# Later exps of q and a bank cycle of four in chunk 0 of an attention-plus-MLP kernel

## The chip, the cores and the metric

The kernel runs on one core of a Trainium2 chip. The metric is the device time of one execution in microseconds (us), as a median over runs. The span in a profile is the same execution without its launch, about 2 us shorter than its time.

## The reference, cut to what matters

```python
# attention, per batch b of 8 and head h of 8, S = 576, D = 64
q_s = softmax(q, axis=-1)            # exp, row sum, divide
k_s = softmax(k, axis=2)
kv  = einsum('bhsd,bhse->bhde', k_s, v)
x   = einsum('bhsd,bhde->bhse', q_s, kv)     # 4608 tokens x 512
# MLP
h   = x @ w_in                        # 512 -> 2048
out = (h * sigmoid(h)) @ w_out        # 2048 -> 512
```

Inputs and output are float32; the kernel multiplies in fp16 and bf16.

## The kernel before

The tokens go through in nine chunks. Chunk 0 makes 16 blocks of 128 features; each block is 8 matmuls into a set of two PSUM banks, then a tanh on ScalarE and a multiply on VectorE which frees the set. There are four sets, named by their first bank: 4, 0, 2 and 6.

```python
WIDE = (4, 0, 2, 6) * 3 + (4, 2, 0, 6)          # bank set of block 0..15

def wide_silu(fb):                               # tanh on ScalarE, multiply on VectorE
    bank = WIDE[fb]
    silu(0, fb, PS[:, bank:bank + 2, 0:S // 2], GTS[0][:, fb, :]..., S)
...
wide_mm(0, (0, 1))                               # first halves of blocks 0, 1, 2 ahead of
xt_evac(0, 1, 6, 0, 320, 0, nc.scalar)           # the second half of x
xt_evac(0, 1, 2, 0, 256, 320, nc.vector)
wide_mm(1, (0, 1))
wide_mm(2, (0, 1))
...
# plan(u, f): f is issued ahead of unit u; units 0..15 are the blocks of chunk 0, b1 = 16
plan(9,  lambda: (load_w2(8, 12), exp_q(1, 0, 0, 1)))
plan(10, lambda: (exp_q(1, 0, 1, 2), qsum_pair(1, 0)))      # qsum_pair: two adds on GpSimd
plan(12, lambda: (exp_q(1, 1, 0, 1), qsum_end(1, 0)))       # qsum_end: reduction on VectorE
plan(13, lambda: (exp_q(1, 1, 1, 2), qsum_pair(1, 1), qnorm(1, 0, nc.gpsimd)))
plan(b1, lambda: (qsum_end(1, 1), qnorm(1, 1, nc.vector)))
...
# joining batch 1: v is cast, k^T v ("kv") multiplied, scaled by VectorE, multiplied with q
plan(b1 + 3, lambda: (ws_op(1, 1), ws_op(2, 1)))            # ws_op: sums of w_in blocks, VectorE
plan(b1 + 4, lambda: ws_op(3, 1))
plan(b1 + 5, lambda: (vcast(1, 1, nc.scalar, 0, 1), vcast(1, 1, nc.vector, 1, 2)))
plan(b1 + 6, lambda: ws_op(4, 1))
plan(b1 + 7, lambda: kv_both(1))                            # kv matmuls, reciprocal, scaling
plan(b1 + 8, lambda: xt(1, 0))                              # "the kv product": q times scaled kv
```

Units from b1 on are the second product, which reads w_out in 16 blocks of 128 rows.

The softmax here doesn't subtract the row's maximum and nothing guards it: scores larger than these inputs give would overflow.

## Time and profile before

| | before |
|---|---|
| median of 3 runs | 261.32 us (261.06 to 261.46) |
| span, TensorE busy | 260.3 us, 251.3 us |
| longest wait of TensorE between the start of chunk 0 and the last stage | 0.8 us near 28 us, for a multiply of VectorE |

A timeline line reads: start in us, length in us, engine, source line, operation, output <- input, shapes, count; in brackets the idle time of the engine before it and what ended it. Some names: PS is the PSUM, sg a tanh's result, GT the product of VectorE's multiply, qt and vt the loaded q and v, eq the exp of q, vaug the cast v, kvn the scaled kv, WS a weight sum. The lines themselves stand in the prediction below.

### The profile page before, as it was taken

To read this page: it belongs to the slowest core of one execution; us is meant where nothing else is said; L and a number is where in the kernel's file an instruction comes from. 1 tells how busy PE (TensorE), PEld (TensorE's weight loads), DVE (VectorE), ACT (ScalarE), POOL (GpSimd) and SP (SyncE) were. 2 spreads that over 40 slices of the span, in tenths; PEclk is the share of its full clock that TensorE was granted. 3 is DMA by queue.
4 is the path that set the end of the run, shared out by engine and by line. 5 is a ranking of instruction groups with operands and counts; after the bars stand their busy time and mean duration, and the time that the engine had idled before them with its cause. 6 is when DMAs were issued, how large, how long until landed. Compare 5 with 4: busy or idle time off the path is not lost.

```text
span 260.3 us, 6411 instructions
## 1 busy us (share of the span) xinstructions
PE 251.3 (97%) x2732; PEld 203.4 (78%) x2732; DVE 208.0 (80%) x268; ACT 187.5 (72%) x212; POOL 65.8 (25%) x63
## 2 busy tenths in 40 slices
PE   8799899999999999999999999999999999999992
PEld 3467656656888888888888888888888888888881
DVE  2867797998997999799979997999798548855932
ACT  5765978998993899489948995799573848484610
POOL 1743791650460306030603060306000000000003
PEclk9999999999999999999999999999999999999999
DMA  6999999679999585956694869530433003300624
GB/s 247 335 196 297 302 320 330 260 159 393 271 343 230 140 246 191 232 128 170 268 249 112 229 216 213 139 83 3 91 81 83 3 0 82 81 3 1 140 64 121
DMA packets 35964, 45.89 MB, mean 176 GB/s; under 512 B 16208, under 2 KB 21008, under 8 KB 35936
## 3 DMA queue, kind: packets, MB, share of 16 engines
q1 hardware_dynamic: 29568, 33.69, 47.5%
q0 software_dynamic: 6128, 11.60, 17.3%
q8 instruction: 21, 0.34, 0.6%
q10 hardware_dynamic: 240, 0.20, 0.2%
q14 instruction: 7, 0.06, 0.1%
HBM read 36.70 MB, written 9.44 MB: 177 GB/s over the span
## 4 chain that ended last, share of the span: by engine, by line
PE 66%; DVE 3%; POOL 1%; issue 0%; ACT 0%; POOLq 0%; DVEq 0%; ACTq 0%
PE PS L477 34%; PE PS L377 30%; PE PS L234 2%; DVE h L355 1%; PE PS L195 1%; DVE GT L451 1%; POOL out_dram L740 1%; DVE zq L154 0%; DVE ow L725 0%; ACT sc L493 0%; DVE ow L497 0%; DVE rzq L158 0%; POOLq L856 0%; DVE kvn L208 0%; DVE rz L206 0%
## 5 line engine op out<-in xcount | busy, mean ns | idle before, releaser
L355 DVE TENSOR_TENSOR h<-PS,h 128x1024 f32<-128x1024 f32 (+1 forms) x45 | 54.0, 1199 | 12.7 <-ACT h L89 6.3
L477 PEld LDWEIGHTS <-GT 128*128 128x128 f16 x512 | 49.6, 98 | 6.9 <-issue 1.2
L377 PEld LDWEIGHTS <-WS 128*128 128x128 f16 x480 | 46.8, 98 | 6.2 <-issue 0.5
L477 PE MATMUL PS<-W,GT 128*128 128x256 f16 x384 | 49.1, 273 | 0.0
L377 PE MATMUL PS<-XS,WS 128*128 128x256 f16 (+1 forms) x360 | 46.3, 272 | 0.1
L361 ACT ACTIVATE GT<-h 128x1024 f16<-128x1024 f32 (+1 forms) x45 | 46.1, 1047 | 0.1
L89 ACT COPY h<-PS 128x1024 f32<-128x1024 f32 (+1 forms) x35 | 35.1, 1003 | 13.1 <-PE PS L377 12.6
L163 POOL TENSOR_TENSOR eq<-eq,rzq 128x1152 bf16<-128x1152 bf16 x13 | 27.7, 2133 | 53.7 <-DVE rzq L158 53.3
L477 PEld LDWEIGHTS <-S 128*128 128x128 f16 x384 | 37.2, 98 | 5.2 <-issue 1.0
L377 PEld LDWEIGHTS <-W 128*128 128x128 f16 x360 | 34.7, 98 | 4.7 <-issue 0.2
L477 PE MATMUL PS<-T,S 128*128 128x256 f16 x256 | 32.7, 273 | 0.0
L377 PE MATMUL PS<-XT,W 128*128 128x256 f16 (+1 forms) x240 | 29.5, 272 | 0.0
L361 ACT ACTIVATE GT<-PS 128x1024 f16<-128x1024 f32 (+1 forms) x15 | 15.2, 1016 | 18.9 <-PE PS L377 18.9
L91 POOL CAST vaug<-vt 128x1152 bf16<-128x1152 f32 x12 | 14.8, 1240 | 44.4 <-DMA vt<-in_v_dram 36.0
L108 ACT ACTIVATE eq<-qt 128x1152 bf16<-128x1152 f32 (+1 forms) x18 | 19.1, 1059 | 3.3 <-DMA qt<-in_q_dram 3.2
L740 POOL DMA_DIRECT2D out_dram<-ow x5 | 2.7, 547 | 72.3 <-DVE ow L725 72.3
L113 ACT ACTIVATE ek<-kt 128x1152 bf16<-128x1152 f32 x16 | 18.4, 1153 | 1.4 <-DMA kt<-in_k_dram 1.4
L154 DVE TENSOR_REDUCE zq<-eq 128x18 f32<-128x1152 bf16 x12 | 16.1, 1345 | 3.8 <-ACT eq L108 3.8
L267 PE MATMUL PS<-XT,W 128*128 128x288 f16 x128 | 16.2, 286 | 0.8 <-DVE GT L257 0.8
L477 PE MATMUL PS<-W,S 128*128 128x256 f16 x128 | 16.5, 273 | 0.0
L497 DVE SCALAR_TENSOR_TENSOR ow<-PS,sc 128x512 f32<-128x512 f32 x7 | 4.8, 692 | 14.4 <-ACT sc L493 14.4
L267 PEld LDWEIGHTS <-W 128*128 128x128 f16 x128 | 12.4, 98 | 4.6 <-issue 1.2
(79 smaller groups left out, 346.7 us busy)
## 6 DMA issues: line engine op xcount, KB each, us to landing
out_dram<-ow SPq DMA_DIRECT2D x64, 128.0 KB, 2.4
qt<-in_q_dram SPq DMA_DIRECT2D x12, 576.0 KB, 4.7
kt<-in_k_dram SPq DMA_DIRECT2D x12, 576.0 KB, 5.6
vt<-in_v_dram SPq DMA_DIRECT2D x12, 576.0 KB, 5.4
qt<-in_q_dram POOLq DMA_DIRECT2D x4, 576.0 KB, 10.8
kt<-in_k_dram POOLq DMA_DIRECT2D x4, 576.0 KB, 13.8
vt<-in_v_dram POOLq DMA_DIRECT2D x4, 576.0 KB, 12.9
W<-in_moe_w_out_dram POOLq DMA_DIRECT2D x4, 512.0 KB, 15.2
```

The costliest lines, as they stand in the source:

```text
L89: eng.copy(out=o, in_=i)
L91: eng.tensor_copy(o, i)
L108: nc.scalar.activation(out=half(st[b]["eq"], cc)[:, :, g0:g1], in_=jgd(b, "qt", cc)[:, :, g0:g1], func=ACT.Exp)
L113: nc.scalar.activation(out=half(ek, cc), in_=jgd(b, "kt", cc), func=ACT.Exp)
L154: nc.vector.reduce_sum(out=z, in_=e, axis=AX.X)
L163: eng.tensor_tensor(out=e, in0=e, in1=r[:, :, :, None].to_broadcast([128, J, 2, D]), op=ALU.mult)
L267: nc.tensor.matmul(out=PS[:, WIDE[fb] + n, 0:S // 2], lhsT=W1[:, c, fb * 128:(fb + 1) * 128], rhs=XTS[0][:, c, n * (S // 2):(n + 1) * (S / ...
L355: nc.vector.tensor_tensor(out=four(t, i), in0=group_bank(t, True), in1=four(t, i), op=ALU.add)
L361: nc.scalar.activation(out=group_out(t, f, n), in_=x, func=ACT.Silu, scale=1.0 / XS)
L377: nc.tensor.matmul(out=PS[:, bank + p // 2, (p % 2) * HT:(p % 2) * HT + width(t)], lhsT=a[:, c, p * 128:(p + 1) * 128], rhs=bb[:, c, 0:wid ...
L477: nc.tensor.matmul(out=PS[:, bank, m * HN:(m + 1) * HN], lhsT=a[:, fc, m * 128:(m + 1) * 128], rhs=bb[:, fc, :], start=(first and fc == 0) ...
L740: eng.dma_start(out=rows(last, th * HT + a * 128 + i * P)[:, n * HN:(n + 1) * HN], in_=o[i * P:(i + 1) * P, :],)
```

## The change

The intent: free TensorE of its one stall in chunk 0. The four exps of batch 1's q go later between the tanhs, the last one behind the last tanh; the row sums of the second half go from GpSimd to VectorE; and all blocks use the bank sets in one cycle of four, so that a block always waits for the block four back.

```diff
-    WIDE = (4, 0, 2, 6) * 3 + (4, 2, 0, 6)
+    WIDE = (4, 2, 0, 6) * 4
...
-    wide_mm(1, (0, 1))
     wide_mm(2, (0, 1))
...
-        wide_mm(fb, range(2 if fb < 3 else 0, NC))
+        wide_mm(fb, range(2 if fb in (0, 2) else 0, NC))
...
-    plan(9, lambda: (load_w2(8, 12), exp_q(1, 0, 0, 1)))
-    plan(10, lambda: (exp_q(1, 0, 1, 2), qsum_pair(1, 0)))
-    plan(12, lambda: (exp_q(1, 1, 0, 1), qsum_end(1, 0)))
-    plan(13, lambda: (exp_q(1, 1, 1, 2), qsum_pair(1, 1), qnorm(1, 0, nc.gpsimd)))
-    plan(14, lambda: (load(2, "qt", q, 0, nc.gpsimd), load(2, "qt", q, 1, nc.gpsimd)))
+    plan(9, lambda: load_w2(8, 12))
+    plan(10, lambda: exp_q(1, 0, 0, 1))
+    plan(11, lambda: (exp_q(1, 0, 1, 2), qsum_pair(1, 0)))
+    plan(14, lambda: (exp_q(1, 1, 0, 1), qsum_end(1, 0), qnorm(1, 0, nc.gpsimd)))
+    plan(15, lambda: qsum(1, 1, 0))
...
-    plan(b1, lambda: (qsum_end(1, 1), qnorm(1, 1, nc.vector)))
+    plan(b1, lambda: (exp_q(1, 1, 1, 2), qsum(1, 1, 1), qnorm(1, 1, nc.vector)))
+    plan(b1, lambda: (load(2, "qt", q, 0, nc.gpsimd), load(2, "qt", q, 1, nc.gpsimd)))
```

## The prediction

> **What bounds the kernel now.** I read the page first (engines, slices), then TensorE's waits, then the timelines of chunk 0 and of the first units after it, engine by engine, then which instruction waits for which transfer. On the page, TensorE is the bound:
>
> ```profile
> PE 251.3 (97%) x2732; PEld 203.4 (78%) x2732; DVE 208.0 (80%) x268; ACT 187.5 (72%) x212; POOL 65.8 (25%) x63
> PEclk9999999999999999999999999999999999999999
> ```
>
> At full clock throughout it is idle for only 260.3 - 251.3 = 9.0 us. The table by stretches gives 46.08 busy us of 47 in 15 to 62 us, where the whole change lies, and 179.92 of 180 in 62 to 242 us. So only some 0.9 us is there to be had, and nearly all of it is one gap, in the timeline of TensorE:
>
> ```profile
> 15.06 13.12 PE L267 MATMUL PS<-XT,W 128*128 128x288 f16 x104
> 28.96 3.10 PE L267 MATMUL PS<-XT,W 128*128 128x288 f16 x24 [0.78 <-DVE GT L257]
> 31.94 3.61 PE L414 MATMUL PS<-W,GT 128*128 128x512 f16 x16
> ```
>
> A feature block of chunk 0 (fb) is 8 such matmuls, so x104 are blocks 0 to 12, and the gap stands before block 13. Block 13 writes bank set 2; in the old cycle block 10 used it, only three blocks back. Its tanh is late because ScalarE stands in its queue for q of batch 1 and then does exps between the tanhs:
>
> ```profile
> 24.30 0.65 ACT L256 ACTIVATE sg<-PS 128x576 f32<-128x576 f32 x1 [0.33 <-PE PS L267]
> 25.79 0.68 ACT L108 ACTIVATE eq<-qt 128x576 bf16<-128x576 f32 x1 [0.84 <-DMA qt<-in_q_dram]
> 26.38 0.63 ACT L256 ACTIVATE sg<-PS 128x576 f32<-128x576 f32 x1
> 26.91 0.67 ACT L108 ACTIVATE eq<-qt 128x576 bf16<-128x576 f32 x1
> 27.48 1.18 ACT L256 ACTIVATE sg<-PS 128x576 f32<-128x576 f32 x2
> ```
>
> The rows from 26.38 hold the tanhs of blocks 9, 10 and 11: block 9's matmuls were done for a tanh at about 24.30 + 0.98 = 25.28 us. The second place to read is where batch 1's attention joins, some 10 us later:
>
> ```profile
> 37.53 0.68 DVE L328 TENSOR_TENSOR WS<-W 128x1024 f16<-128x1024 f16 x1
> 38.28 0.68 ACT L89 CAST vaug<-vt 128x576 bf16<-128x576 f32 x1 [0.30 <-DMA vt<-in_v_dram]
> 38.28 0.76 DVE L91 CAST vaug<-vt 128x576 bf16<-128x576 f32 x1
> 39.07 0.81 PE L195 MATMUL PS<-vaug,ek 64*64 64x65 bf16 x72
> 39.28 0.68 DVE L328 TENSOR_TENSOR WS<-W,WS 128x1024 f16<-128x1024 f16 x1
> 40.01 0.18 DVE L206 RECIPROCAL rz<-PS 128x4 f32<-128x4 f32 x1
> 40.23 0.49 DVE L208 TENSOR_TENSOR kvn<-PS,rz 128x128 bf16<-128x128 f32 x2
> 40.78 0.38 PE L234 MATMUL PS<-qT,kvn 64*64 64x448 bf16 x4
> ```
>
> ScalarE and VectorE start the two halves of the last v cast in the same instant, 38.28 us, because the transfer has just landed. From there VectorE runs without a pause into the scaled kv, which releases TensorE's product at 40.78 us. TensorE's own work before it (72 kv matmuls from 39.07, four others from 39.81) ends at that moment too: two chains tie.
>
> **What the Trainium skill says.** (1) "ScalarE: Activation LUTs", section "Table sets: the hidden batching unit": exp and tanh are in one set. The trace agrees: no ACT_TABLE_LOAD between 15 and 51 us, so moving exps among tanhs costs or saves no load. (2) "SBUF — State Buffer", section "Who interferes with whom": a VectorE instruction with two inputs in SBUF contends with a GpSimd one that reads SBUF; a reduction never does. The trace agrees:
>
> ```profile
> L163 DVE TENSOR_TENSOR eq<-eq,rzq x3: 1357/1357/1711, 7.2 to 34.2; 128x1152 bf16<-128x1152 bf16 x3
> ```
>
> The 1711 ns is the one at 34.23 us, beside GpSimd's own normalization (32.61 to 34.73 us). (3) "DMA: Bandwidth & Descriptors", section "Queues, rings and completion order": on each DMA engine descriptors are consumed in ring order. Here batch 1's two v loads were issued at 21.97 and 24.93 us by GpSimd and landed about 36.8 and 38.2 us; the DMA share is above 1 all that time. They stand behind earlier loads and not behind their own issue.
>
> **The change part by part.** *The start.* Before, four matmuls each of blocks 0, 1 and 2 ran ahead of the second half of x; now only of 0 and 2, as block 1 has bank set 2, evacuated last. Cost of a matmul: 0.98 / 8 = 0.122 us. Block 0's second half would come at 15.06 + 8 x 0.122 = 16.04 us, but it needs a weight load which, from GpSimd's issue at 16.59 us that waits for the same transfer, and the 0.25 us by which GpSimd trails other engines at such releases (19.43 against 19.18, 26.05 against 25.79), landed about 16.34. Then 24 matmuls: 16.34 + 2.94 = 19.28 us for block 4, against 19.18, where the next weight load held it before. Cost: 0.1 us.
>
> *The gap.* Block 13 now waits for block 9, whose tanh (25.38 us) precedes every exp and whose multiply ends about 26.8 us, long before 28.1. Block 14 waits for 10: tanh 26.5, multiply done about 28.0, needed 29.1. Block 15 waits for 11: done 29.1, needed 30.1. No stall. Expected start of block 13: 28.06 + 0.1 = 28.16 instead of 28.96, so the second product begins about 31.14 us instead of 31.94: **0.8 us ahead**.
>
> *The tail on ScalarE and VectorE.* Two GpSimd adds go (1.29 + 0.80 us) and one 0.45 us reduction with them; VectorE gets two of 128x576 at 0.70 (the pair at 46.17 us takes 1.40). ScalarE: tanh 14 at 30.40, tanh 15 at 31.25, the last exp 31.78 to 32.46. VectorE, at the spacings of before (0.68 a multiply, 0.30 a reciprocal): multiply 13 at 29.97, reduction 30.65, reciprocal 31.14, multiply 14 31.32, reduction 32.0, multiply 15 32.7, reduction 33.4, reciprocal 34.1, normalization 34.4. That is 0.2 us later than 34.23, but GpSimd's normalization, freed by the reciprocal, now runs about 31.5 to 33.6 us and is out of the way: 1.36 us instead of 1.71. VectorE is free at about 35.7 instead of 35.87.
>
> *Where the lead goes.* TensorE's first transposes come at about 34.4 us (GpSimd done 33.6), the second at 35.75 (VectorE done 35.76): no loss to speak of. The first half of kv can then start at about 38.2. But its second half needs the v cast, which needs the v load, and that one is neither issued earlier nor made smaller. VectorE waits until 38.28 as before, casts, copies, does its weight sum from 39.28 and reaches the reciprocal at 40.01. So the product of 40.78 us stays at 40.78, and all that follows stays where it was. Sum: -0.8 us at 32 us, given back as waiting between 38 and 41 us, **net 0.0 to -0.1 us**.
>
> **Rivals.** *The lead survives* (-0.4 to -0.8 us, 260.5 to 260.9): this needs the v load to land earlier. Its queue has the same transfers in front in the same order, so I give it 0.15. *It gets worse* (+0.1 to +0.6 us): VectorE's queue is full from 30 to 41 us; if the two reductions or the normalization take longer than worked out, the weight sums slide past 38.28, then the v cast starts late and every 0.1 us shows in full at 40.78. There is about 0.2 us of room by my sums, and the q and w_out loads of later chunks, issued 1 us earlier, could take bandwidth from v, though they are behind it in the ring: 0.2. *The start costs more*: if the weight load of 16.34 lands later, the lead shrinks, but the v load still hides it: no effect on the time. *An early block of w_out* (the fifth, first used at 35.89 us) may not have landed at 35.0: this too is swallowed before 38.28.
>
> **Range and chances.** The three runs of before span 261.06 to 261.46 us around 261.32. Zero net with a lean to the survival of a little of the lead gives 261.2 us; full survival is about 260.5 and the bad case about 261.8, so 260.5 to 261.7 us at 8 in 10. Two per cent is 5.2 us, six times what the gap is worth, and no mechanism above costs that: faster 0.01, same 0.98, slower 0.01.
>
> **What would show it.** Right: no wait of TensorE for GT near 28 us; the second product about 0.8 us earlier; VectorE's normalization near 1.36 us; then a new wait or idle stretch of TensorE between 38 and 41 us; casts of v again at about 38.28 and the product with kv at about 40.8 us. Wrong: casts of v clearly before 38 us, which would make the time fall by as much, or starting later than the landing because VectorE is still in its weight sums, which would make it rise; or a stall that remains before blocks 13 to 15.

## The result

The changed kernel took 261.16 us as a median (260.88 to 261.89, 4 runs), the kernel before 261.39 (261.06 to 261.50, 4 runs). The ratio is 0.9998, with a 95% interval of 0.9975 to 1.002. Ratios here are the mean time of one kernel's runs over that of the other's of the same rounds, so they are not quite the ratio of the medians quoted beside them. The time lies in the predicted range.

TensorE's timeline of the changed kernel answers to the three lines of before with the gap:

```profile
15.24 15.86 PE L267 MATMUL PS<-XT,W 128*128 128x288 f16 x128
30.93 3.62 PE L414 MATMUL PS<-W,GT 128*128 128x512 f16 x16
...
35.25 1.02 PE L414 MATMUL PS<-W,GT 128*128 128x512 f16 x4 [0.20 <-DMA W<-in_moe_w_out_dram]
...
38.43 1.09 PE L195 MATMUL PS<-vaug,ek 64*64 64x65 bf16 x72
...
40.58 0.38 PE L234 MATMUL PS<-qT,kvn 64*64 64x448 bf16 x4
```

All 128 matmuls of chunk 0 now run in one piece, and the second product starts at 30.93 us instead of 31.94. ScalarE shows why the wait is gone: the tanh of block 9 (25.25 us) now stands ahead of the first exp, and that exp waits for no load.

```profile
25.25 0.65 ACT L256 ACTIVATE sg<-PS 128x576 f32<-128x576 f32 x1 [0.33 <-PE PS L267]
25.80 0.68 ACT L108 ACTIVATE eq<-qt 128x576 bf16<-128x576 f32 x1
26.37 0.64 ACT L256 ACTIVATE sg<-PS 128x576 f32<-128x576 f32 x1
26.90 0.68 ACT L108 ACTIVATE eq<-qt 128x576 bf16<-128x576 f32 x1
27.47 1.37 ACT L256 ACTIVATE sg<-PS 128x576 f32<-128x576 f32 x2
```

But the kv product starts at 40.58 instead of 40.78. The lead of 1.0 us has shrunk to 0.2 within 10 us. VectorE's timeline shows where:

```profile
37.13 0.68 DVE L328 TENSOR_TENSOR WS<-W 128x1024 f16<-128x1024 f16 x1
38.22 0.76 DVE L91 CAST vaug<-vt 128x576 bf16<-128x576 f32 x1 [0.41 <-DMA vt<-in_v_dram]
38.89 0.41 DVE L91 COPY qT<-PS 128x512 bf16<-128x512 bf16 x1
39.23 0.68 DVE L328 TENSOR_TENSOR WS<-W,WS 128x1024 f16<-128x1024 f16 x1
39.82 0.18 DVE L206 RECIPROCAL rz<-PS 128x4 f32<-128x4 f32 x1
```

VectorE is free 0.41 us before the last half of v lands. Then follow cast, copy, the fourth weight sum and the reciprocal, back to back. This is the predicted picture. VectorE's normalization is short, as worked out, because GpSimd's (31.41 to 33.53 us) is over before it starts:

```profile
L163 DVE TENSOR_TENSOR eq<-eq,rzq x3: 1357/1357/1358, 7.2 to 34.2; 128x1152 bf16<-128x1152 bf16 x3
```

**How to compare two profiles to a tenth of a microsecond.** A profile is one execution, and the first loads do not land at the same moment in each. In the thirteen profiles the first block of chunk 0 starts between 14.79 and 15.71 us, which alone is a spread of 0.92 us in the time. So I cut each span into four parts: the start of the first block (A), from there to the second product (B), from there to the kv product (C), and the rest (D). In before these are 15.06, 31.94 - 15.06 = 16.88, 40.78 - 31.94 = 8.84 and 260.3 - 40.78 = 219.5 us. D is 219.3 to 219.6 in all thirteen profiles: within these 0.3 us, nothing after the kv product depends on any of these edits. What an edit does is in B and C. A is taken as chance, as no edit changes what runs before the first block, but for the tile filled at the start in the three kernels marked as wrong. The column v is the start of ScalarE's last v cast, counted from A: ScalarE always waits for the load there, so it tells when the load landed.

| profile | A | B | C | B + C | v |
|---|---|---|---|---|---|
| before | 15.06 | 16.88 | 8.84 | 25.72 | 23.22 |
| changed | 15.24 | 15.69 | 9.65 | 25.34 | 22.98 |

So B fell by 1.19 us and C grew by 0.81.

### The profile page after: what moved, and what is told of

Its sections match the earlier page's. It is cut to its first block, busy times and chain, and to the rows that moved or that the text cites. A ratio compares the mean times of both kernels' runs of the same rounds, so it can differ in the third digit from the quotient of the medians.

```text
span 260.1 us, 6409 instructions
## 1 busy us (share of the span) xinstructions
PE 252.4 (97%) x2732; PEld 203.9 (78%) x2732; DVE 208.7 (80%) x269; ACT 187.7 (72%) x212; POOL 63.7 (25%) x61
## 4 chain that ended last, share of the span: by engine, by line
PE 72%; DMA 12%; DVE 6%; ACT 5%; issue 2%; SPq 1%; POOL 1%; POOLq 0%; ACTq 0%; DVEq 0%
PE PS L477 34%; PE PS L377 30%; DMA vt<-in_v_dram 9%; PE PS L267 3%; DMA qt<-in_q_dram 3%; PE PS L234 2%; DVE T L461 2%; DVE h L355 1%; PE PS L195 1%; DVE zq L156 1%; SPq L97 1%; ACT eq L108 1%; POOL out_dram L739 1%; PE PS L414 1%; PE PS L285 1%
## 5 line engine op out<-in xcount | busy, mean ns | idle before, releaser
L377 PEld LDWEIGHTS <-W 128*128 128x128 f16 x360 | 34.7, 98 | 4.7 <-issue 0.2
L91 POOL CAST vaug<-vt 128x1152 bf16<-128x1152 f32 x12 | 14.8, 1240 | 44.3 <-DMA vt<-in_v_dram 34.4
L414 PE MATMUL PS<-W,GT 128*128 128x512 f16 x64 | 15.6, 379 | 0.2 <-DMA W<-in_moe_w_out_dram 0.2
```

The costliest lines, as they stand in the source:

```text
L91: eng.tensor_copy(o, i)
L377: nc.tensor.matmul(out=PS[:, bank + p // 2, (p % 2) * HT:(p % 2) * HT + width(t)], lhsT=a[:, c, p * 128:(p + 1) * 128], rhs=bb[:, c, 0:wid ...
L414: nc.tensor.matmul(out=PS[:, 2 + tb, :], lhsT=GTS[t % 2][:, fc, tb * 128:(tb + 1) * 128], rhs=W2[:, fc, :], start=(fc == 0), stop=(fc == N ...
```

## The experiments

Four questions: which part of the change removes the gap, what takes the lead back, whether that cost the kernel before anything too, and whether the lead can be kept. All experiments are correct to the reference but for the three marked as wrong. Kernels are compared only within the same rounds. Several expectations name the kv product by the clock; since A alone moves that by up to 0.9 us, they are judged here by C or by B + C.

### The two halves of the change

`cycle_only` is the kernel before with the new `WIDE` and the new start; `exps_only` is the changed kernel with the old ones:

```diff
-    WIDE = (4, 2, 0, 6) * 4
+    WIDE = (4, 0, 2, 6) * 3 + (4, 2, 0, 6)
...
+    wide_mm(1, (0, 1))
...
-        wide_mm(fb, range(2 if fb in (0, 2) else 0, NC))
+        wide_mm(fb, range(2 if fb < 3 else 0, NC))
```

> The kernel before with the bank cycle of four alone (exps where they were). Theory (either half removes the gap; the lead is then swallowed at the v load): block 13 waits for block 9, whose multiply ends about 27.8 us, so no wait of TensorE near 28 us; the second product starts about 31.1 us; the scaled kv product stays at 40.6 to 40.8 us; time within 0.2 us of before. Rival (only the later exps remove the gap): the wait of 0.8 us near 28 us stays.

> The changed kernel with the old bank cycle and the old start (exps late). Theory: block 13 waits for block 10, whose tanh is now at about 26.4 us and whose multiply ends about 27.8 us, so no wait near 28 us either; the kv product again at 40.6 to 40.8 us; time within 0.2 us of before and of the changed kernel. Rival (the cycle is what removes the gap): 0.5 us or more of wait near 28 us stays.

Measured: `cycle_only` 262.10 us against 262.03 of before, ratio 1.0003 (0.9974 to 1.0031); `exps_only` 261.22 us, ratio 0.9974 (0.9941 to 1.0006). TensorE in `cycle_only`:

```profile
15.32 15.90 PE L267 MATMUL PS<-XT,W 128*128 128x288 f16 x128
31.82 3.61 PE L414 MATMUL PS<-W,GT 128*128 128x512 f16 x16 [0.60 <-DVE GT L257]
```

The gap before block 13 is gone, as expected, but it has only moved: the second product starts by writing the banks of block 13, and now waits 0.60 us for that block's multiply. I had expected the second product at 31.1 us and it came at 31.82; on this I was wrong. The exps are still ahead of ScalarE's last tanhs (that of block 13 starts at 30.10 us), and a longer bank cycle lets TensorE run on without making ScalarE any earlier. In `exps_only`, with the old cycle, there is no wait at all:

```profile
15.00 15.85 PE L267 MATMUL PS<-XT,W 128*128 128x288 f16 x128
30.69 3.62 PE L414 MATMUL PS<-W,GT 128*128 128x512 f16 x16
```

Its B is 15.69 us, that of the changed kernel to the hundredth. So the later exps make the whole lead, and the bank cycle and the new start add nothing that these profiles show. (`exps_only` also keeps the changed row sums and the later q loads of batch 2. No run takes these apart, but in before the first GpSimd sum ends at 28.94 us and the first reduction starts at 29.86, too late to cause a wait that ends at 28.96.) Its kv product came at 39.86 us, earlier than I had expected (40.6 to 40.8): the first sign that the lead need not be lost. The time was expected within 0.2 us of before; the median is 0.81 us lower, with an interval that just includes 1.

### Taking the loads away

`b_v_w` and `a_v_w` give a wrong result. Batch 1's casts of v read a tile filled at the start, and the second product reads only the first four blocks of w_out. All transfers are still made, but none can hold these two. `a_v_w` is made from the changed kernel, `b_v_w` from the one before.

```diff
         i = jgd(b, "vt", cc)[:, :, g0:g1, :]
+        if b == 1:
+            i = VF.rearrange("p g (j d) -> p j g d", d=D)[:, :, g0:g1, :]
...
-                rhs=W2[:, fc, :],
+                rhs=W2[:, fc % 4, :],
...
+    VF = GTS[1].rearrange("p f n -> p (f n)")[:, 0:4 * S].bitcast(FP32)...
+    nc.gpsimd.memset(VF, 0.25)
```

> Wrong result on purpose: the kernel before, its casts of batch 1's v read a tile filled at the start and the second product reads only w_out blocks 0 to 3, so neither the v loads nor the later w_out loads can hold anything; all transfers are still made. Theory: before the change TensorE's own work ends with the landings, so nothing is gained: kv product at 40.6 to 40.8 us, time within 0.15 us of before. Rival (the v load already cost time before): clearly faster.

> Wrong result on purpose: the changed kernel with the same two freedoms from the loads. Theory: the lead now survives up to the next limit, VectorE's weight sums: kv product at about 40.2 us instead of 40.6, time 0.3 to 0.5 us below the changed kernel and 0.4 to 0.7 below before. Rival (VectorE's queue holds the end of the stage and the load does not matter): kv product at 40.5 us or later and the time of the changed kernel.

Measured: `b_v_w` 261.91 us, ratio 1.0012 (0.9963 to 1.0061); `a_v_w` 261.24 us, ratio 0.9966 (0.9935 to 0.9997), both against 262.03 of before. In `b_v_w` C is 40.28 - 31.44 = 8.84 us, exactly that of before: there TensorE's own work sets C, and no load cost anything. In `a_v_w` C is 40.24 - 31.09 = 9.15 us: with no load of v or w_out to wait for, 0.31 us of the lead is still given back. (Its B, 15.95 us, is 0.26 above the other changed profiles: a load of w_in held TensorE's weight load at 19.32 us for 0.40 us.) The expected 0.3 to 0.5 us below the changed kernel can't be judged. It was run at another time. VectorE in `a_v_w` (line numbers are two higher there):

```profile
37.30 0.68 DVE L330 TENSOR_TENSOR WS<-W 128x1024 f16<-128x1024 f16 x1
37.90 0.75 DVE L91 CAST vaug<-GT 128x576 bf16<-128x576 f32 x1
38.56 0.41 DVE L91 COPY qT<-PS 128x512 bf16<-128x512 bf16 x1
38.89 0.68 DVE L330 TENSOR_TENSOR WS<-W,WS 128x1024 f16<-128x1024 f16 x1
39.49 0.17 DVE L208 RECIPROCAL rz<-PS 128x4 f32<-128x4 f32 x1
```

It works without a pause. So the load is only a part of what takes the lead; VectorE's own queue is the other.

### The changed kernel again

> The changed kernel once more, on the chip of the next three. Theory: no wait near 28 us, kv product between 39.9 and 40.7 us according to when the v load lands in the profiled execution; time 0 to 0.4 us below before. Rival (nothing at all survives): equal to before within 0.1 us.

> The changed kernel a third time, to see how far its profile repeats. Theory after eight runs: kv product 25.0 to 25.3 us behind the first block of chunk 0 (before: 25.3 to 25.7); time 0.2 to 0.4 us below before, which one set of rounds can hardly tell from none. Rival: no difference at all.

Measured, on two different chips: 260.92 us against 261.21 of before, ratio 0.9990 (0.9972 to 1.0008), and 261.31 against 262.02, ratio 0.9976 (0.9949 to 1.0003). C was 9.32 and 9.15 us. In `after_third` B + C is 24.84 us, below the expected 25.0 to 25.3, and the median is 0.71 us below before where 0.2 to 0.4 was expected. In `after_third` ScalarE's cast stands at 37.37 us and VectorE gets to its own only at 37.78, straight from the third weight sum:

```profile
37.19 0.68 DVE L328 TENSOR_TENSOR WS<-W 128x1024 f16<-128x1024 f16 x1
...
37.37 0.67 ACT L89 CAST vaug<-vt 128x576 bf16<-128x576 f32 x1 [0.31 <-DMA vt<-in_v_dram]
37.78 0.75 DVE L91 CAST vaug<-vt 128x576 bf16<-128x576 f32 x1
...
38.78 0.69 DVE L328 TENSOR_TENSOR WS<-W,WS 128x1024 f16<-128x1024 f16 x1
...
39.38 0.18 DVE L206 RECIPROCAL rz<-PS 128x4 f32<-128x4 f32 x1
```

Here the load did not hold VectorE at all, and C is that of `a_v_w`. In `after_third`, VectorE is ready for its cast 37.78 - 15.29 = 22.49 us after A. The load landed 22.08 us after A here, 22.66 in `after_again`, 22.98 in the first profile: C rises with it, 9.15, 9.32, 9.65.

### Moving the fourth weight sum

If the sum between the cast and the reciprocal is what remains, moving it behind the scaling must bring the kv product forward in the changed kernel, and not in the one before. The sum is first read at about 52 us.

```diff
-    plan(b1 + 6, lambda: ws_op(4, 1))
-    plan(b1 + 8, lambda: t_op(1, nc.vector))
+    plan(b1 + 8, lambda: (ws_op(4, 1), t_op(1, nc.vector)))
```

> The changed kernel with one weight sum on VectorE (the fourth of its group, first needed some 12 us later) moved from before to behind the scaled kv. Theory: once the v load has landed, that sum of 0.6 us is what the product still waits for, so the reciprocal starts right behind the kv matmuls, 0.3 us after landing-relative place of the changed kernel is saved (reciprocal about 1.3 us after the start of the last v cast instead of 1.6); then the ninth block of w_out, landing about 40.6 us, is the next limit: time 0.2 to 0.3 us below after_again. Rival (TensorE's own work or the load alone holds the product): no difference.

> The kernel before with the same move of that weight sum. Theory: before the change the kv matmuls end as late as that sum, so the move gives at most 0.1 us. Rival (the sum was a cost of its own all along): as large a gain as in a_ws4.

> Wrong result on purpose: a_v_w (no wait for v or for later w_out blocks) with that weight sum moved too. Theory: now neither load nor sum holds, so the kv product follows TensorE's own work, at 39.9 to 40.0 us, and the whole lead of 0.7 to 0.8 us shows: time 0.6 to 0.9 us below before. Rival (a further limit stands behind these): kv product no earlier than in a_v_w, 40.2 us.

Measured, all against 261.21 us of before: `a_ws4` 260.78 us, ratio 0.9986 (0.9968 to 1.0005); `b_ws4` 261.33, ratio 1.0001 (0.9985 to 1.0018); `a_v_w_ws4`, wrong, 260.74, ratio 0.9982 (0.9963 to 1.0). VectorE in `a_ws4`:

```profile
38.21 0.74 DVE L91 CAST vaug<-vt 128x576 bf16<-128x576 f32 x1
38.87 0.41 DVE L91 COPY qT<-PS 128x512 bf16<-128x512 bf16 x1
39.61 0.18 DVE L206 RECIPROCAL rz<-PS 128x4 f32<-128x4 f32 x1 [0.32 <-PE PS L195]
```

TensorE's kv matmuls in `a_ws4`:

```profile
38.55 0.94 PE L195 MATMUL PS<-vaug,ek 64*64 64x65 bf16 x72
```

VectorE's reciprocal now waits 0.32 us for TensorE's kv matmuls, so no weight sum holds it any more. C is 40.38 - 31.41 = 8.97 us, and 8.98 in `a_v_w_ws4`, where the loads are out of the way too. So in this execution the load cost nothing once the sum was moved, because the cast needs it at 22.5 us after A and it landed at 22.48. In `b_ws4` C is 8.85 us, as in before: there the sum was free. The step in C has the expected sign, but is 0.2 us and not 0.3: the reciprocal comes 1.40 us behind the start of the cast, 1.60 in the changed kernel, 1.3 expected. `a_v_w_ws4` was expected 0.6 to 0.9 us below before, with the whole lead of 0.7 to 0.8 us; its median is 0.47 below, and its B + C (24.67 in the table below) 0.6 us below those of the kernels made from before. The time is not resolved either, as the median of `a_ws4` lies 0.14 us below `after_again` where I had expected 0.2 to 0.3. The ninth block of w_out, which I had named as the next limit, landed at about 40.6 us and was first used at 40.70: no wait.

> The changed kernel with the weight sum moved, again. Theory: kv product 24.6 to 24.8 us behind the first block, time 0.4 to 0.7 us below before and about 0.3 below the changed kernel. Rival: the first result (0.14 us below the changed kernel's median) was chance.

> Late exps and the moved weight sum, with the old bank cycle and the old start. Theory (the late exps alone make the lead, the cycle adds nothing): kv product 24.6 to 24.8 us behind the first block and the time of a_ws4. Rival (the cycle of four is part of the gain): a wait of TensorE in chunk 0 and a time nearer to before.

`exps_ws4` is `exps_only` with the same move. Measured, against 262.02 of before: `a_ws4_again` 261.26 us, ratio 0.9968 (0.9941 to 0.9995); `exps_ws4` 261.10, ratio 0.9960 (0.9933 to 0.9987). Both intervals lie below 1. Against the changed kernel of the same rounds (261.31) the medians are 0.05 and 0.21 us lower, which these rounds cannot tell from none; I had expected 0.3. Against before, the median of `a_ws4_again` is 0.76 us lower (expected 0.4 to 0.7). In the profiles it is plain:

| profile | A | B | C | B + C | v |
|---|---|---|---|---|---|
| cycle_only | 15.32 | 16.50 | 8.84 | 25.34 | 22.55 |
| b_v_w | 14.97 | 16.47 | 8.84 | 25.31 | none |
| b_ws4 | 14.86 | 16.42 | 8.85 | 25.27 | 22.56 |
| after_again | 14.79 | 15.69 | 9.32 | 25.01 | 22.66 |
| after_third | 15.29 | 15.69 | 9.15 | 24.84 | 22.08 |
| exps_only | 15.00 | 15.69 | 9.17 | 24.86 | 22.51 |
| a_v_w | 15.14 | 15.95 | 9.15 | 25.10 | none |
| a_ws4 | 15.71 | 15.70 | 8.97 | 24.67 | 22.48 |
| a_ws4_again | 14.96 | 15.68 | 9.09 | 24.77 | 22.58 |
| exps_ws4 | 15.30 | 15.69 | 8.98 | 24.67 | 22.07 |
| a_v_w_ws4 | 14.85 | 15.69 | 8.98 | 24.67 | none |

## Why the prediction was right, and where it was not

**The gap and the lead: right in mechanism, small in size.** Block 13's wait went. The lead at the second product was predicted as 0.8 us. Between the two profiles it was 1.0 us by the clock and 1.19 us in B. The profile of before had an unlucky execution: in `b_v_w` and `b_ws4`, whose chunk 0 is the same as in before, B is 16.47 and 16.42 us, so the lead over these is 0.73 to 0.78 us. The traces show where the difference comes from. The first exp, which waits for the q load, starts 10.73 us after A in before, and 10.33, 10.28 and 10.35 us in `b_v_w`, `b_ws4` and `cycle_only`; the second product follows 6.14 to 6.15 us behind it in all four. So the gap is in part a wait for q, handed on by ScalarE and VectorE, and its size depends on when q lands; with the late exps, no profile shows a wait for q there. How much of the gap would stay if q landed early, no run tells.

That the cause was the exps was said. But the step on the gap rested on the new cycle ("Block 13 now waits for block 9"), and that was not needed: in `exps_only` block 13 still waits for block 10 and finds it done. That the cycle alone would not do was not seen, and `cycle_only` showed it.

**The start: not seen.** A cost of 0.1 us was predicted for the shorter start. B is 15.69 us with the new start and with the old one (`exps_only`). The predicted B was 31.14 - 15.06 = 16.08 us: it also kept a wait of before, where TensorE's weight load for block 4 was held 0.34 us at 19.18 us by a load of w_in, and this wait is absent from the changed profile.

**The tail on VectorE: right.** Normalization predicted at 34.4 us, measured 34.20; its length predicted as 1.36, measured 1.36; VectorE free for the weight sums at 35.7, measured 35.47. The fifth block of w_out held TensorE for 0.20 us, as one rival had it, and that was swallowed too.

**Where the lead goes: right for the profile, too strong as a rule.** The step said that the product of 40.78 us "stays at 40.78" because the v load pins it. In that profile the casts came at 38.22 (predicted 38.28), the kv product at 40.58, and C took back 0.81 us. The 0.20 us between 40.78 and 40.58 is 0.06 from the load and 0.14 from a misread line: the prediction has VectorE run "without a pause" to the reciprocal in before, but there the reciprocal started 0.73 us after the fourth weight sum (39.28, 40.01), and 0.59 after it in the changed kernel (39.23, 39.82). So in before it waited some 0.14 us for the kv matmuls; the two chains did not quite tie, and TensorE's was the longer, as `b_v_w` also shows. Above all, the runs show two holds one behind the other. VectorE's queue gives back 0.31 us even with no load to wait for (9.15 - 8.84, `a_v_w`); its last part before the reciprocal is the fourth weight sum, and moving that one returns 0.17 us (9.15 - 8.98, `a_v_w` against `a_v_w_ws4`). The other 0.14 us (8.98 - 8.84) stands in the kv matmuls: they begin 7.14 us behind the second product in `a_ws4` and 7.13 in before, but take 0.94 us instead of 0.81. In `a_v_w_ws4`, where they take 0.94 us too, the single starts in the trace show a pause of 0.16 us before the 38th, the first that reads VectorE's half of the last v cast; in before there is none. That cast stands behind the third weight sum. The late landing of v adds between nothing and 0.5 us (9.65 - 9.15), by execution. Where v lands early, 0.3 to 0.5 us of the lead survives: B + C is 24.84 and 25.01 us in the two further profiles, against 25.27 to 25.34 in the three kernels made from before. The rival "the lead survives", given 0.15, was thus partly true.

**The time: within the range.** Predicted 261.2, measured 261.16. Agreement to 0.04 us is luck, as the four runs spread over 1.0 us. Three sets of rounds gave ratios of 0.9998, 0.9990 and 0.9976, and none of their intervals excludes 1. A gain of 0.3 to 0.5 us, as the two further profiles have it, fits all three, but the times alone do not show it.

**What stays open.** Why A and the landing of v differ between executions was not examined. The pause of 0.16 us in the kv matmuls is read from traces; no run moved the third weight sum to test it. `exps_ws4` is the version to keep: it is faster than before with an interval below 1 (by 0.4%) and does without the new bank cycle and start. Its profile accounts for 0.6 us of that (B + C of 24.67 against 25.27 to 25.34), and it is not shown to be faster than the changed kernel.

## What to carry to other kernels

Before removing a stall, look for the next meeting point of the engines, and ask of each partner whether it would have been ready earlier: what is hidden behind TensorE today becomes the wait tomorrow, and a cheap instruction standing in an in-order queue ahead of the one that matters costs nothing until then. When a profile's start shifts by more than the effect, cut the span at events that all versions share and compare the parts; here B was 15.68 to 15.70 us in eight of the nine profiles with late exps, where times scattered by 1 us. A longer buffer cycle does not cure an engine that is behind with its work: it moves the wait to the next user of the buffer.

## What the Trainium skill lacked or had wrong

- "SBUF — State Buffer", section "Who interferes with whom": its rule of blocking holds here. VectorE's normalization took 1357 ns alone, 1711 ns when it began 0.5 us before GpSimd's ended (before) and 2041 ns when it began 0.8 us before that (`cycle_only`, 33.79 against 32.49 + 2.12 = 34.61 us). The loss falls short of a full block by nearly the same amount both times, 0.35 of 0.50 and 0.68 of 0.82 us, which the section does not mention; as GpSimd's ends are rough in these profiles, the 0.14 to 0.15 us may be theirs. VectorE's reductions beside GpSimd's normalization took 0.74 and 0.75 us in the changed kernel, and all four in before 740 to 745 ns, of which two ran with GpSimd idle, so "never contends" holds.
- "DMA: Bandwidth & Descriptors", section "Queues, rings and completion order": no figure for how far the landing of the same load varies between executions. Here the v load ranged over 0.90 us in three executions of the changed kernel (22.08 to 22.98 us after the first block), more than the whole effect of the change. The sentence on ring order that the prediction cites stands in that section's paragraph on loads issued by SyncE and ScalarE; for loads issued by GpSimd, as here, the section says nothing of order. In before the two v loads landed in order of issue, about 36.8 and 38.2 us.
- "ScalarE: Activation LUTs", section "Table sets: the hidden batching unit": nothing wrong; exps and tanhs were mixed in every order tried without a table load between them.
